# Top-32 attention and a top-1 expert layer: routing the first three batches sooner, ranks beside the one-hot rows, four stacked rows for a slot's choice

## The chip, the cores and the metric

One core of one Trainium2 chip runs the whole program in one launch. The metric is the device time of an execution in microseconds (us), taken as the median of three runs. Engines are named as the profile names them: PE (TensorE, matmuls), DVE (VectorE), ACT (ScalarE), POOL (GpSimd) and SP (SyncE, which here only issues DMAs).

## The reference

```
scores = q @ k^T / sqrt(64)                  # 8 batches, 8 heads, 576 x 576
kth    = 32nd largest score of each row
scores = where(scores >= kth, scores, -1e9)
attn   = softmax(scores)                     # exp(s - max) / (sum + 1e-9)
x      = (attn @ v) as 4608 tokens x 512     # heads side by side

logits = x @ w_gate + modality_bias[modality_id]   # 8 experts
e_idx  = argmax(logits);  gate = softmax(logits)[e_idx]
out    = gate * (relu(x @ w1[e_idx]) @ w2[e_idx])  # w1 512 x 1024, w2 1024 x 512
```

All of it is in float32. A token's expert depends on the attention output of all eight heads, so the tokens of a batch can be routed only when its 36 tiles are done.

## The kernel before

The attention is cut into 32 pairs (a batch and two heads) of 9 query tiles, 288 tiles in all, 36 to a batch. One loop of 310 steps pipelines them: step i multiplies the scores of tile i+2 on PE (`S`, line 383) and transposes the probabilities of tile i-9 (`T`, line 491), while DVE looks for the 32 largest of the tiles in between (lines 395 to 446) and forms the masked probabilities (line 457, or in the first 48 tiles lines 464 and 470 with POOL). PE multiplies by v for three tile roles of a pair (line 519). One 36-step stretch is called a batch period here.

When the attention of a batch is complete, some steps later, small operations of the router are dealt out over the steps, a handful to each step: reciprocals, logits, one-hot rows of the chosen experts (`route`, lines 616 to 622), then in a later step the ranks of the tokens in their experts' lists (`ranks`, lines 599 to 606, PE), the destinations, and the scatter of the x rows to lists in DRAM by five indirect DMAs on POOL (`send`, line 610). `PAUSE` in a list ends the step's share. `done` marks the batch as seen.

The experts work on slots of 256 rows. `sched` chooses the next expert and its rows on DVE (lines 672 to 699, ending in the row `sei`), SP reads `sei` into registers (lines 703 and 706) and issues the DMA of the rows, `xg` (line 707), and of the weights (lines 728 and 732). PE transposes `xg` (line 774 when the list of waiting work is empty, line 786 when the slot before is still running) and does 16 units of x @ w1 (line 796) and 16 of h @ w2 (line 808) in full fp32. These units stand in one list, `moe`; a budget for each step (`STEP`, the costs in `COST`, the cap `CAP`) says how many are taken into PE's instructions behind the attention's. Thirteen slots go into the loop. Slots 0 to 5 are chosen by the long form of `sched` (partly filled lists), 6 to 12 by the short form (`whole`). Where there is no expert work, `keep_warm` (line 960) puts in six bf16 matmuls that nobody reads.

After the loop the tail does six slots one after the other with three fp32r matmuls for each fp32 one (lines 1057 and 1073). Their operands are split into high and low parts on ACT and DVE (lines 1012 and 1013); the choices there are of the long form.

All instructions of an engine run in the order in which they are written, so this planning in Python at build time sets what waits behind what. `arrange` orders the DVE operations within a step by modelled durations; the small operations are one chain there. In steps near the routing of the first seven batches up to `RNQ` of the choice's and `SNQ` of the router's small operations go into one step.

Of the kernel before, what the change touches and what calls it, by code (L numbers as in the profile page):

```python
# [9 lines left out]
FT = mybir.dt.float32  # L10
# [19 lines left out]
NW = 3  # L30
# [14 lines left out]
TL = LR + 2  # L45
# [11 lines left out]
QO = 0  # L57
PJ0 = (1, 2, 3)
FAST = 7
RXQ = (2, 3, 3, 4, 4)  # L60
SNQ, RNQ = 12, 12
RLF = (0, 1)
RXF = (3, 4, 5, 6, 7)
EZP = 1
# [11 lines left out]
def kernel(  # L76
# [132 lines left out]
    base = const.tile([128, E], FT, name="base")  # L209
    er = const.tile([128, 2, E], FT, name="er")  # L210
    G.iota(er[:, 0, :], pattern=[[1, E]], base=0, channel_multiplier=0, allow_small_or_imprecise_dtypes=True)
    roff = er[:, 1, :]
    zc = const.tile([1, 2], FT, name="zc")
    G.memset(zc[:, 0:1], 0.0)
    G.memset(zc[:, 1:2], float(ZROW))
# [371 lines left out]
    def route(lg, bias, oh, x5b, wait=0):  # L587
# [20 lines left out]
        def send(c):  # L608
# [12 lines left out]
            lambda: V.tensor_tensor(oh[:, 0:4, :], key[:, 0:4, :], bc(km)[:, 0:4, :], op=OP.is_equal),  # L621
            lambda: V.tensor_tensor(oh[:64, 4, :], key[:64, 4, :], km[:64, 4:5].to_broadcast([64, E]),
                                    op=OP.is_equal),
            PAUSE,
            *[PAUSE] * wait,
            lambda: A.activation(ez, z, AF.Exp),
            ranks,
            PAUSE,
            lambda: V.tensor_reduce(sm, ez, axis=AX.X, op=OP.add),
            lambda: V.tensor_scalar(sm, sm, EPS, None, op0=OP.add),  # L630
# [25 lines left out]
    def sched(s, whole):  # L656

        o = {"w1": {}}  # L660
        SL[s] = o
        t8 = lambda nm: const.tile([128, E], FT, name=nm)
        av_, key, oh, m8, jk, a8 = t8("s_av"), t8("s_key"), t8("s_oh"), t8("s_m8"), t8("s_jk"), t8("s_a8")
        sc = const.tile([128, 6], FT, name="s_sc")
        at, n_, full, r0, r1 = (sc[:, x:x + 1] for x in range(1, 6))
        i = s % 2
        ei = sei[i]
        mk = smk[i]
        ft = const.tile([128, 2], FT, name="s_ft")
        dot = lambda x, y, w=1.0: V.scalar_tensor_tensor(jk, oh, w, y, op0=OP.mult, op1=OP.mult, accum_out=x)  # L670
        pick = [
            lambda: V.tensor_tensor(av_, base, roff, op=OP.subtract),
            lambda: V.scalar_tensor_tensor(key, av_, float(E), rev, op0=OP.mult, op1=OP.add),
            lambda: V.max(m8, key),
        ]
        if whole:
            both = const.tile([128, 2, E], FT, name="s_er")
            ea = const.tile([128, 2], FT, name="s_ea")
            pick += [lambda: V.tensor_scalar(full, m8[:, 0:1], float(SLOT * E), None, op0=OP.is_gt),
                     lambda: V.tensor_scalar(oh, key, m8[:, 0:1], full, op0=OP.is_equal, op1=OP.mult),  # L680
                     lambda: V.tensor_tensor(both, er, oh[:, None, :].to_broadcast([128, 2, E]), op=OP.mult),
                     lambda: V.tensor_reduce(ea, both, axis=AX.X, op=OP.add),
                     lambda: V.tensor_tensor(ei, ea[0:1, :], zc, op=OP.add)]
        else:
            pick += [lambda: V.tensor_scalar(oh, key, m8[:, 0:1], None, op0=OP.is_equal),
                     lambda: dot(n_, av_),
                     lambda: V.scalar_tensor_tensor(a8, base, -float(SLOT), eoff, op0=OP.add, op1=OP.max),
                     lambda: V.tensor_tensor(a8, a8, roff, op=OP.min),
                     lambda: dot(at, a8),
                     lambda: dot(r0, roff),  # L690
                     lambda: dot(r1, base),
                     lambda: V.tensor_scalar(ft, pos, at, r0, op0=OP.add, op1=OP.is_ge),
                     lambda: V.tensor_scalar(mk, pos, at, r1, op0=OP.add, op1=OP.is_lt),
                     lambda: V.tensor_tensor(mk, mk, ft, op=OP.mult),
                     lambda: dot(sc[:, 0:1], ie),
                     lambda: V.tensor_scalar(ei, sc[0:1, 0:2], float(ZROW), None, op0=OP.add)]
        done = [lambda: V.scalar_tensor_tensor(roff, oh, float(SLOT), roff, op0=OP.mult, op1=OP.add)] if whole else [
            lambda: V.tensor_scalar(n_, n_, float(SLOT), None, op0=OP.min),
            lambda: V.scalar_tensor_tensor(roff, oh, n_, roff, op0=OP.mult, op1=OP.add),
        ]  # L700

        def which():
            o["e"] = SP.value_load(ei[:, 0:1], min_val=0, max_val=E - 1)

        def rows():
            a = SP.value_load(ei[:, 1:2], min_val=0, max_val=ZROW)
            r = SP.dma_start(xg, xs[ds(a, SLOT), :].rearrange("(p t) w -> p t w", t=2)).ins
            o["rows"] = True
# [282 lines left out]
    for x in range(QL):  # L991
# [3 lines left out]
            qk(0, 0, qbd[0])  # L995
            keep_warm(KP)
        sevac(x)
    keep_warm(NW)
    ok = lambda x: 0 <= x < NT
    early = lambda u: u < EARLY and u % 3 != 2  # L1000
    dn_of = lambda u: den[(u // 36) % 2][:, (u // 9) % HP, role(u):role(u) + 1]
# [109 lines left out]
    for i in range(LAST):  # L1111
# [59 lines left out]
        if 0 <= b1 < B:  # L1171
            if r == 0:
                chore.extend(recip(b1, den[b1 % 2]))
# [10 lines left out]
                    xrow(b1, c, xTs(b1), x5)  # L1184
                    cost += COST["xrow"]
            if r == rl[1] + (1 if early_route(b1) else 2):
                steps, store = route(lgb[b1 % 2], bias_all[:, b1], ohb[b1 % 2], x5, int(FAST <= b1 < B - 1))
# [277 lines left out]
```

## Time and profile before

| | us |
|---|---|
| median of 3 runs (lowest, highest) | 1211.64 (1211.17, 1212.91) |
| profiled execution | 1209.28 |
| span in its trace | 1207.6 |
| PE busy | 1157.0 (96%) |
| DVE busy | 1104.1 (91%) |
| ACT busy | 983.4 (81%) |
| POOL busy | 677.7 (56%) |

The span is the stretch between the first and the last instruction in the trace; the rest of the execution's time lies around it. A busy share is a mean over stages, so whichever engine is short has to be read from the windows. In a timeline a row's bracket tells how long the engine sat idle before it and on whom it waited. `SPq` is SP's queue of DMA issues. The granted clock (PEclk) is given as a share of TensorE's full 2.4 GHz; its lower level is 1.2 GHz.

### The profile page before, as it was taken

The page shows a single profiled execution, that of the slowest core. Times are in us where ns is not written, and L with a number is a line of the kernel's source. Part 1 is how long each engine was busy: PE and PEld are TensorE (multiplying, and loading weights), DVE is VectorE, ACT ScalarE, POOL GpSimd, SP SyncE. Part 2 cuts the span into 40 slices and gives each one's busy share as a digit, 9 for nine tenths or more (in the row PEclk, how much of TensorE's full clock was granted, in tenths as well). Part 3 has the DMA queues.
Part 4 walks back from the last instruction along what each step waited for, and adds up shares of the span by engine and source line. Part 5 has one row for each costly group of instructions (what it writes and reads, how often), then busy time and mean ns, then how long its engine had stood idle before and what let it go on. Part 6 is the DMA issues. An engine that isn't in the chain of part 4 may idle for free.

```text
span 1207.6 us, 28111 instructions
## 1 busy us (share of the span) xinstructions
PE 1157.0 (96%) x7920; PEld 906.5 (75%) x7920; DVE 1104.1 (91%) x5562; ACT 983.4 (81%) x2015; POOL 677.7 (56%) x1256
## 2 busy tenths in 40 slices
PE   8889979999999998999999999999999999999998
PEld 6666767778677876878687777868787777589987
DVE  7999999999999999999999999999998999486772
ACT  5999978998888986998899899989998888355652
POOL 6888875564755565565656576556655666121011
PEclk9999999999999998999999999999999999999999
DMA  5653358663586637664675657665675653277750
GB/s 125 174 163 88 88 127 236 191 167 88 153 241 152 164 104 220 175 174 123 174 215 149 168 148 196 168 160 147 183 192 145 177 156 126 83 269 237 261 198 22
DMA packets 204324, 197.10 MB, mean 163 GB/s; under 512 B 104413, under 2 KB 151533, under 8 KB 204160
## 3 DMA queue, kind: packets, MB, share of 16 engines
q1 hardware_dynamic: 196880, 175.92, 54.0%
q0 software_dynamic: 6080, 19.00, 4.3%
q8 instruction: 66, 1.08, 0.4%
q14 instruction: 98, 0.80, 0.2%
q10 hardware_dynamic: 1200, 0.30, 0.1%
HBM read 118.63 MB, written 24.23 MB: 118 GB/s over the span
## 4 chain that ended last, share of the span: by engine, by line
PE 59%; DVE 31%; ACT 5%; issue 2%; DMA 1%; POOL 0%; SPq 0%; POOLq 0%; ACTq 0%; DVEq 0%
PE E L796 11%; PE E L808 11%; PE X L519 8%; DVE cand L395 8%; PE S L383 7%; PE T L491 6%; DVE mg L437 5%; DVE P L457 5%; PE X L1073 5%; PE X L1057 4%; DVE cand L406 2%; DVE cand L407 2%; PE E L1057 1%; DVE mg L408 1%; PE X L317 1%
## 5 line engine op out<-in xcount | busy, mean ns | idle before, releaser
L395 DVE MAX8 cand<-Ssb 128x8 f32<-128x96 f32 x1728 | 388.1, 244 | 1.8 <-ACT Ssb L388 1.8
L433 POOL TENSOR_TENSOR y<-Ssb,K 128x576 f32<-128x576 f32 x288 | 368.7, 1280 | 30.5 <-ACT K L427 30.1
L383 PE MATMUL S<-ks,qs 128*128 128x288 f32 x992 | 221.1, 345 | 18.7 <-ACT Ssb L388 12.9
L427 ACT ACTIVATE K<-Ssb,n 128x576 bf16<-128x576 f32 x288 | 229.9, 798 | 7.3 <-POOL y L433 6.9
L388 ACT ACTIVATE Ssb<-S 128x576 f32<-128x576 f32 x284 | 187.8, 661 | 53.5 <-PE S L383 23.8
L437 DVE MAX8 mg<-y 128x8 f32<-128x576 f32 x288 | 213.3, 741 | 4.2 <-POOL y L433 4.2
L796 PE MATMUL E<-xgT,w1b 128*128 128x256 f32 x832 | 201.1, 384 | 2.6 <-ACT hT L800 1.5
L451 ACT ACTIVATE ex<-Ssb,sm 128x576 f32<-128x576 f32 x256 | 202.3, 790 | 0.0
L383 PEld LDWEIGHTS S<-ks,qs 128*128 128x128 f32 x992 | 152.1, 190 | 66.8 <-issue 26.2
L457 DVE SCALAR_TENSOR_TENSOR P<-Ssb,kth,ex 128x576 f32<-128x576 f32 x230 | 193.7, 842 | 6.8 <-ACT ex L451 5.6
L499 ACT ACTIVATE PT<-T 128x640 f32<-128x640 f32 (+1 forms) x288 | 193.5, 672 | 5.8 <-PE T L491 5.8
L808 PE MATMUL E<-w2b,hT 128*128 128x512 f32 x416 | 194.2, 595 | 0.5 <-ACT hT L800 0.2
L491 PE MATMUL T<-idf,P 128*128 128x128 f32 x1152 | 169.5, 274 | 7.2 <-ACT P L476 6.6
L796 PEld LDWEIGHTS E<-xgT,w1b 128*128 128x128 f32 x832 | 151.0, 190 | 29.5 <-ACT hT L800 7.4
L480 POOL TENSOR_SCALAR spare<-P 1x1 f32<-1x1 f32 x230 | 41.7, 181 | 196.6 <-DVE mg L406 166.7
L519 PE MATMUL X<-PT,vm 128*64 128x256 f32 (+1 forms) x1536 | 147.3, 334 | 1.2 <-DVE x L553 1.2
L491 PEld LDWEIGHTS T<-idf,P 128*128 128x128 f32 x1152 | 137.2, 140 | 13.8 <-ACT P L476 10.7
L519 PEld LDWEIGHTS X<-PT,vm 128*64 128x64 f32 x1536 | 89.1, 138 | 46.4 <-issue 12.5
L420 POOL TENSOR_SCALAR n<-mg 128x1 f32<-128x1 f32 x288 | 71.2, 247 | 92.5 <-DVE mg L408 70.1
L808 PEld LDWEIGHTS E<-w2b,hT 128*128 128x128 f32 x416 | 73.3, 190 | 61.9 <-issue 58.1
L1079 POOL DMA_INDIRECT out_dram<-ot,tk x12 | 12.3, 1022 | 101.9 <-ACT ot L1078 101.9
L427 ACT ACTIVATION_READ_ACCUMULATOR K<-Ssb,n 128x1 f32 x288 | 63.7, 221 | 0.0
(234 smaller groups left out, 2166.1 us busy)
## 6 DMA issues: line engine op xcount, KB each, us to landing
w1b<-in_moe_w_dram SPq DMA_DIRECT2D x76, 512.0 KB, 5.7
w2b<-in_moe_w_dram SPq DMA_DIRECT2D x76, 512.0 KB, 5.1
ks<-st SPq DMA_DIRECT2D x62, 288.0 KB, 4.3
ks<-st SPq DMA_DIRECT2D x62, 256.0 KB, 4.5
qs<-st SPq DMA_DIRECT2D x124, 128.0 KB, 5.3
xg<-xs SPq DMA_DIRECT2D x19, 516.0 KB, 4.1
vm<-in_v_dram SPq DMA_DIRECT2D x32, 256.0 KB, 5.1
km<-in_k_dram SPq DMA_DIRECT2D x63, 128.0 KB, 3.6
```

The costliest lines, as they stand in the source:

```text
L383: PE.matmul(ps[:, hf, :288], l, m, start=(n == 0), stop=(n == len(terms) - 1))
L395: return [lambda s=s: V.max(c[:, s * 8:s * 8 + 8], T[i]["S"][:, bnd[s]:bnd[s + 1]]) for s in range(NSUB)]
L427: A.activation(t["K"], t["S"], AF.Sign, scale=2.0 ** -24 - 1.0, bias=t["n"][:, 1, i % 3:i % 3 + 1], accum_out=t["n"][:, 0, i % 3:i % 3 + 1])
L433: G.tensor_tensor(t["y"], t["S"], t["K"], op=OP.mult)
L437: V.max(t["mg"][:, i % 3, 24:32], t["y"])
L451: A.activation(t["ex"], t["S"], AF.Exp, bias=t["s"][:, i % 3:i % 3 + 1])
L457: V.scalar_tensor_tensor(t["P"], t["S"], kth[:, i:i + 1], t["ex"], op0=OP.is_ge, op1=OP.mult, accum_out=dn)
L491: PE.transpose(T[i]["pt"][:, x, :], (Pm if c == 4 else Pb[c % 2])[:, h * 512 + x * 128:h * 512 + x * 128 + 128], idf)
L499: A.activation(o, T[i]["pt"][:, :n], AF.Copy)
L519: PE.matmul(o.rearrange("p (a b) -> p a b", a=2) if j < 8 else o, l, r, start=(c == 0), stop=(c == 4))
L796: PE.matmul(ps[:, f % 2], w1b[:, c, f * 128:(f + 1) * 128], xgT[:, c, :], start=(c == 0), stop=(c == KC - 1))
L808: PE.matmul(o["py"], hT[:, f, t * 128:(t + 1) * 128], w2b[:, f, :], start=(f == 0), stop=(f == FC - 1))
```

## The change

For the first three batches (`SOON`) the router's schedule counts from one step earlier, the v product of a batch's last role-7 tile is executed at once and not queued, the preparation of k in the second pair of batches 1 to 3 moves from the second step of the pair to the third, the ranks follow the one-hot rows without a pause and stand ahead of the softmax of the gate, and the scatters are handed out by the third x row's step. `RNQ` is 18 where it was 12. In the long form of `sched`, four rows (expert number, list start, list end, last start) are stacked in `er`, so that one product with the one-hot row and one reduction give what five dot products gave. The six warm-up matmuls before the loop are gone.

```
-SNQ, RNQ = 12, 12
+SOON = 3
+SNQ, RNQ = 12, 18
...
+    er = const.tile([128, 4, E], FT, name="er")
+    roff, base, last = (er[:, x, :] for x in range(1, 4))
...
             lambda: V.tensor_tensor(oh[:64, 4, :], key[:64, 4, :], km[:64, 4:5].to_broadcast([64, E]),
                                     op=OP.is_equal),
-            PAUSE,
-            *[PAUSE] * wait,
-            lambda: A.activation(ez, z, AF.Exp),
-            ranks,
+            *[PAUSE] * (wait + 1 - soon),
+            *[lambda: A.activation(ez, z, AF.Exp), ranks][::-1 if soon else 1],
             PAUSE,
...
+        sums = [lambda: V.tensor_tensor(both, er[:, :w], oh[:, None, :].to_broadcast([128, w, E]), op=OP.mult),
+                lambda: V.tensor_reduce(ea, both, axis=AX.X, op=OP.add),
+                lambda: V.tensor_tensor(ei, ea[0:1, 0:w:w - 1], zc, op=OP.add)]
...
-            pick += [lambda: V.tensor_scalar(oh, key, m8[:, 0:1], None, op0=OP.is_equal),
-                     lambda: dot(n_, av_),
-                     lambda: V.scalar_tensor_tensor(a8, base, -float(SLOT), eoff, op0=OP.add, op1=OP.max),
-                     lambda: V.tensor_tensor(a8, a8, roff, op=OP.min),
-                     lambda: dot(at, a8),
-                     lambda: dot(r0, roff),
-                     lambda: dot(r1, base),
-                     lambda: V.tensor_scalar(ft, pos, at, r0, op0=OP.add, op1=OP.is_ge),
-                     lambda: V.tensor_scalar(mk, pos, at, r1, op0=OP.add, op1=OP.is_lt),
-                     lambda: V.tensor_tensor(mk, mk, ft, op=OP.mult),
-                     lambda: dot(sc[:, 0:1], ie),
-                     lambda: V.tensor_scalar(ei, sc[0:1, 0:2], float(ZROW), None, op0=OP.add)]
+            pick += [lambda: V.scalar_tensor_tensor(last, base, -float(SLOT), eoff, op0=OP.add, op1=OP.max),
+                     lambda: V.tensor_scalar(oh, key, m8[:, 0:1], None, op0=OP.is_equal),
+                     lambda: V.tensor_tensor(last, last, roff, op=OP.min)] + sums
...
-            lambda: V.tensor_scalar(n_, n_, float(SLOT), None, op0=OP.min),
+            lambda: V.tensor_scalar(n_, r1, r0, float(SLOT), op0=OP.subtract, op1=OP.min),
+            lambda: V.tensor_scalar(ft, pos, at, r0, op0=OP.add, op1=OP.is_ge),
             lambda: V.scalar_tensor_tensor(roff, oh, n_, roff, op0=OP.mult, op1=OP.add),
+            lambda: V.tensor_scalar(mk, pos, at, r1, op0=OP.add, op1=OP.is_lt),
+            lambda: V.tensor_tensor(mk, mk, ft, op=OP.mult),
...
-    keep_warm(NW)
     ok = lambda x: 0 <= x < NT
...
         part = (PREP if p else PREP0).get(j)
+        if 1 <= p // HP <= SOON and p % HP == 1 and j in (1, 2):
+            part = PREP.get(1) if j == 2 else None
...
-        b1, r = divmod(i - (TL + 2), 36)
+        b1, r = divmod(i - (TL + 1), 36)
+        if b1 > SOON:
+            b1, r = divmod(i - (TL + 2), 36)
         b1 -= 1
+        soon = b1 < SOON
...
-            if r == max(rl[1], rx[4]) + (1 if early_route(b1) else 2):
+            if r == (rx[2] + 1 if soon else max(rl[1], rx[4]) + (1 if early_route(b1) else 2)):
...
-            if role(u) == 7:
+            if role(u) == 7 and not (u % 36 == 35 and u // 36 < SOON):
                 avs.extend(f)
```

What this does to the plan, read from the two builds: for batch 0 the choice of slot 0 stands in step 50 (52 and 53 before), the scatters in steps 50 to 52, the rows' DMA in step 52 (54) and PE's first use of them in step 53 (55), and POOL's product of line 470 no longer stands between the fourth scatter and the fifth. For batch 1 the choice and the rows of slot 2 stand in step 90 (92 and 93), for batch 2 those of slot 4 in step 126 (128 and 129). From there on the list of expert work runs ahead of the kernel before by 4 to 13 elements (a unit is an element).

The first place is SP's queue at the choice of slot 4. In the kernel before, the copies of the next pair's keys (`ks`) stand ahead of the loads of `sei`:

```order
290 L333 DMA ks<-st 64x2x576 x2
291 L333 DMA ks<-st 64x2x512
292 L333 DMA ks<-st 64x2x64
293 L333 DMA ks<-st 64x2x512
294 L333 DMA ks<-st 64x2x64
295 L703 TENSOR_LOAD sei_132
296 L703 ISA x2
297 L706 TENSOR_LOAD sei_132
298 L706 ISA x2
299 L707 ISA
300 L707 DMA xg<-xs 128x1032
```

Now:

```order
292 L699 TENSOR_LOAD sei_132
293 L699 ISA x2
294 L700 ISA
295 L700 DMA xg<-xs 128x1032
296 L721 ISA
297 L721 DMA w1b<-in_moe_w_dram 128x4x256
298 L721 ISA
299 L721 DMA w1b<-in_moe_w_dram 128x4x256
300 L721 ISA
301 L721 DMA w1b<-in_moe_w_dram 128x4x256
302 L333 DMA ks<-st 64x2x576 x2
303 L333 DMA ks<-st 64x2x512
```

The six `ks` issues have moved behind the rows' DMA and three loads of w1.

The second place is PE in step 165, just after slot 6 has been chosen in step 164 (both kernels choose it there). Before, the step's rows are S, T, the transposes of q (line 317) and three units of line 808:

```order
1554 L383 MATMUL S<-ks,qs 128x288 x4
1555 L491 MATMUL T<-idf,P_120 128x128 x4
1556 L317 MATMUL X<-idf,qm 128x128 x4
1557 L808 MATMUL E<-w2b,hT 128x512 x3
1558 L383 MATMUL S<-ks,qs 128x288 x4
1559 L491 MATMUL T<-idf,P_120 128x128 x5
1560 L296 MATMUL X<-st,nid 128x512
1561 L808 MATMUL E<-w2b,hT 128x512 x3
1562 L383 MATMUL S<-ks,qs 128x288 x4
1563 L491 MATMUL T<-idf,P_119 128x128 x4
```

Now (line 801 was 808, line 779 was 786):

```order
1512 L383 MATMUL S<-ks,qs 128x288 x4
1513 L491 MATMUL T<-idf,P_120 128x128 x4
1514 L317 MATMUL X<-idf,qm 128x128 x4
1515 L801 MATMUL E<-w2b,hT 128x512 x2
1516 L779 MATMUL X<-idf,xg 128x128 x4
1517 L801 MATMUL E<-w2b,hT 128x512
1518 L383 MATMUL S<-ks,qs 128x288 x4
```

The first transposes of `xg` for slot 6 stand in step 165 behind two units; before, they stand in step 170.

The third place is PE from the last x rows of batch 7 (line 552) into the tail. Before:

```order
2203 L552 MATMUL X<-idf,xT 128x128 x4
2204 L808 MATMUL E<-w2b,hT 128x512
2205 L552 MATMUL X<-idf,xT 64x128 x4
2206 L786 MATMUL X<-idf,xg 128x128 x4
2207 L808 MATMUL E<-w2b,hT 128x512 x7
2208 L1028 MATMUL X<-idf,xg 128x128 x8
2209 L808 MATMUL E<-w2b,hT 128x512
2210 L1057 MATMUL X<-xgh,w1h 128x256
```

Now (lines 1020 and 1049 were 1028 and 1057):

```order
2160 L552 MATMUL X<-idf,xT 128x128 x4
2161 L801 MATMUL E<-w2b,hT 128x512
2162 L552 MATMUL X<-idf,xT 64x128 x4
2163 L801 MATMUL E<-w2b,hT 128x512 x5
2164 L1020 MATMUL X<-idf,xg 128x128 x8
2165 L1049 MATMUL X<-xgh,w1h 128x256
```

Three units and one set of transposes fewer stand there, and one unit more is gone from the steps ahead of it. On ACT the split of `xg` now stands behind the copy of the last result `ot` and a third split of w1; before it stood ahead of that copy, behind three splits of w1.

## Rows read from the trace of the kernel before

**Rows 1.** The page, parts 1 and 4: busy time; shares of the last chain.

```profile
PE 1157.0 (96%) x7920; PEld 906.5 (75%) x7920; DVE 1104.1 (91%) x5562; ACT 983.4 (81%) x2015; POOL 677.7 (56%) x1256
...
PE 59%; DVE 31%; ACT 5%; issue 2%; DMA 1%; POOL 0%; SPq 0%; POOLq 0%; ACTq 0%; DVEq 0%
```

**Rows 2.** Windows, three batch periods: busy us by engine, granted clock (PEclk), DMA share, GB/s.

```profile
273.06:402.12 129.06, 125.89 (x847) 95.60 (x845) 126.46 (x692) 113.17 (x236) 76.24 (x148) 1.00 0.63 164
402.12:535.92 133.80, 128.25 (x847) 98.36 (x846) 129.66 (x691) 112.66 (x235) 76.44 (x146) 0.97 0.60 164
535.92:664.38 128.46, 126.24 (x854) 97.59 (x853) 125.03 (x659) 113.82 (x236) 78.38 (x152) 1.00 0.60 166
```

**Rows 3.** Timeline of POOL, first scatter: start, us, operation, [idle before, releaser].

```profile
173.44 1.27 POOL L470 TENSOR_TENSOR ex<-Ssb,hT 128x576 f32<-128x576 f32 x1 [0.93 <-DVE hT L464]
...
178.84 1.27 POOL L470 TENSOR_TENSOR ex<-Ssb,hT 128x576 f32<-128x576 f32 x1
180.27 1.28 POOL L610 DMA_INDIRECT xs<-x,dest  x1 [0.15 <-issue]
```

**Rows 4.** Chain of waits, first slot: start, us, what.

```profile
180.27 4.88 DMA xs<-x,dest
...
185.16 3.38 DMA xg<-xs
```

**Rows 5.** Timeline of PE, first use of gathered rows.

```profile
188.69 0.63 PE L774 MATMUL E<-idf,xg 128*128 128x128 f32 x4 [0.81 <-DMA xg<-xs]
```

**Rows 6.** Windows around the first slot and around step 130.

```profile
169.92:188.69 18.77, 11.12 (x78) 8.00 (x75) 16.13 (x100) 11.09 (x26) 14.79 (x25) 0.82 0.50 163
180.85:188.69 7.84, 6.48 (x54) 4.62 (x54) 5.27 (x32) 6.04 (x15) 5.64 (x11) 0.78 0.73 254
455.00:460.00 5.00, 3.62 (x16) 3.04 (x18) 4.97 (x31) 2.46 (x5) 3.33 (x5) 0.55 0.99 279
460.00:465.00 5.00, 5.00 (x24) 2.48 (x21) 4.42 (x23) 1.75 (x4) 2.82 (x7) 0.77 1.14 287
```

**Rows 7.** Timeline of all engines, the choice for slot 4.

```profile
445.53 5.47 SPq L333 DMA_DIRECT2D ks<-st  x6
...
449.86 0.14 DVE L696 TENSOR_SCALAR sei<-s_sc 1x2 int32<-1x2 f32 x1
...
452.94 0.37 SPq L707 DMA_DIRECT2D xg<-xs  x1
...
456.38 1.11 PE L786 MATMUL X<-idf,xg 128*128 128x128 f32 x4 [4.91 <-DMA xg<-xs]
```

**Rows 8.** Timeline of all engines, the choice for slot 6.

```profile
581.69 2.84 PE L808 MATMUL E<-w2b,hT 128*128 128x512 f32 x6
581.82 0.15 DVE L683 TENSOR_TENSOR sei<-s_ea,zc 1x2 int32<-1x2 f32 x1
...
583.37 0.35 SPq L707 DMA_DIRECT2D xg<-xs  x1
```

**Rows 9.** Lines of DVE, choice in the first tail slot: busy us, mean ns.

```profile
L670 DVE SCALAR_TENSOR_TENSOR s_jk<-s_oh,base 128x8 f32<-128x8 f32 x1 | 0.2, 169 | 0.0
...
L670 DVE DVE_READ_ACCUMULATOR s_jk<-s_oh,base 128x1 f32 x1 | 0.1, 84 | 0.0
```

**Rows 10.** Lines of DVE, the choice for slot 6, same columns.

```profile
L681 DVE TENSOR_TENSOR s_er<-er,s_oh 128x16 f32<-128x16 f32 x1 | 0.2, 174 | 0.0
```

**Rows 11.** Timeline of PE, start of the tail.

```profile
1054.06 6.28 PE L808 MATMUL E<-w2b,hT 128*128 128x512 f32 x14
...
1061.51 0.68 PE L1057 MATMUL X<-xgh,w1h 128*128 128x256 f32 x1
```

**Rows 12.** Timeline of ACT, start of the tail.

```profile
1054.69 2.94 ACT L1012 ACTIVATE w1h<-w1b 128x1024 fp32r<-128x1024 f32 x3
1060.81 1.08 ACT L1012 ACTIVATE xgh<-X 128x512 fp32r<-128x512 f32 x2 [3.18 <-PE X L1028]
1062.11 0.69 ACT L818 ACTIVATE ot<-E,sgt 128x512 f32<-128x512 f32 x1 [0.21 <-PE E L808]
```

More of the change, by code (lines that the diff above doesn't have):

```diff
@@ L208 @@
     hT = const.tile([128, FC, SLOT], FT, name="hT")
-    base = const.tile([128, E], FT, name="base")
-    er = const.tile([128, 2, E], FT, name="er")
+    er = const.tile([128, 4, E], FT, name="er")
     G.iota(er[:, 0, :], pattern=[[1, E]], base=0, channel_multiplier=0, allow_small_or_imprecise_dtypes=True)
-    roff = er[:, 1, :]
+    roff, base, last = (er[:, x, :] for x in range(1, 4))
     zc = const.tile([1, 2], FT, name="zc")
@@ L585, in logit_rows, with route @@
                 lg[:r, c0:c0 + n, :], lt[:r].rearrange("p c e a h -> p c e (a h)"), axis=AX.X, op=OP.add))
-    def route(lg, bias, oh, x5b, wait=0):
+    def route(lg, bias, oh, x5b, wait=0, soon=False):
         t5 = lambda nm: const.tile([128, 5], FT, name=nm)
@@ L662, in sched @@
         t8 = lambda nm: const.tile([128, E], FT, name=nm)
-        av_, key, oh, m8, jk, a8 = t8("s_av"), t8("s_key"), t8("s_oh"), t8("s_m8"), t8("s_jk"), t8("s_a8")
-        sc = const.tile([128, 6], FT, name="s_sc")
-        at, n_, full, r0, r1 = (sc[:, x:x + 1] for x in range(1, 6))
+        av_, key, oh, m8 = t8("s_av"), t8("s_key"), t8("s_oh"), t8("s_m8")
+        sc = const.tile([128, 2], FT, name="s_sc")
+        n_, full = (sc[:, x:x + 1] for x in range(2))
         i = s % 2
@@ L669, in sched @@
         ft = const.tile([128, 2], FT, name="s_ft")
-        dot = lambda x, y, w=1.0: V.scalar_tensor_tensor(jk, oh, w, y, op0=OP.mult, op1=OP.mult, accum_out=x)
+        w = 2 if whole else 4
+        both = const.tile([128, w, E], FT, name=f"s_er{w}")
+        ea = const.tile([128, w], FT, name=f"s_ea{w}")
+        r0, r1, at = (ea[:, x:x + 1] for x in range(1, 4)) if w == 4 else (None,) * 3
+        sums = [lambda: V.tensor_tensor(both, er[:, :w], oh[:, None, :].to_broadcast([128, w, E]), op=OP.mult),
+                lambda: V.tensor_reduce(ea, both, axis=AX.X, op=OP.add),
+                lambda: V.tensor_tensor(ei, ea[0:1, 0:w:w - 1], zc, op=OP.add)]
         pick = [
@@ L676, in sched @@
         if whole:
-            both = const.tile([128, 2, E], FT, name="s_er")
-            ea = const.tile([128, 2], FT, name="s_ea")
             pick += [lambda: V.tensor_scalar(full, m8[:, 0:1], float(SLOT * E), None, op0=OP.is_gt),
[L680 to L683, printed above, removed]
-        else:
-            pick += [lambda: V.tensor_scalar(oh, key, m8[:, 0:1], None, op0=OP.is_equal),
-                     lambda: dot(n_, av_),
-                     lambda: V.scalar_tensor_tensor(a8, base, -float(SLOT), eoff, op0=OP.add, op1=OP.max),
-                     lambda: V.tensor_tensor(a8, a8, roff, op=OP.min),
-                     lambda: dot(at, a8),
-                     lambda: dot(r0, roff),
-                     lambda: dot(r1, base),
-                     lambda: V.tensor_scalar(ft, pos, at, r0, op0=OP.add, op1=OP.is_ge),
-                     lambda: V.tensor_scalar(mk, pos, at, r1, op0=OP.add, op1=OP.is_lt),
-                     lambda: V.tensor_tensor(mk, mk, ft, op=OP.mult),
-                     lambda: dot(sc[:, 0:1], ie),
-                     lambda: V.tensor_scalar(ei, sc[0:1, 0:2], float(ZROW), None, op0=OP.add)]
@@ L697, in sched @@
+                     lambda: V.tensor_scalar(oh, key, m8[:, 0:1], full, op0=OP.is_equal, op1=OP.mult)] + sums
+        else:
+            pick += [lambda: V.scalar_tensor_tensor(last, base, -float(SLOT), eoff, op0=OP.add, op1=OP.max),
+                     lambda: V.tensor_scalar(oh, key, m8[:, 0:1], None, op0=OP.is_equal),
+                     lambda: V.tensor_tensor(last, last, roff, op=OP.min)] + sums
         done = [lambda: V.scalar_tensor_tensor(roff, oh, float(SLOT), roff, op0=OP.mult, op1=OP.add)] if whole else [
-            lambda: V.tensor_scalar(n_, n_, float(SLOT), None, op0=OP.min),
+            lambda: V.tensor_scalar(n_, r1, r0, float(SLOT), op0=OP.subtract, op1=OP.min),
+            lambda: V.tensor_scalar(ft, pos, at, r0, op0=OP.add, op1=OP.is_ge),
@@ L1186 @@
             if r == rl[1] + (1 if early_route(b1) else 2):
-                steps, store = route(lgb[b1 % 2], bias_all[:, b1], ohb[b1 % 2], x5, int(FAST <= b1 < B - 1))
+                steps, store = route(lgb[b1 % 2], bias_all[:, b1], ohb[b1 % 2], x5, int(FAST <= b1 < B - 1), soon)
                 side.extend(steps)
```

## The prediction

> **What bounds the kernel now.** I read the page first. PE is busy 96% of the span and DVE 91%, and the chain that ended last runs 59% over PE and 31% over DVE [rows 1]. Neither engine is alone, so what an edit is worth depends on the place. The next view is therefore the windows, cut at batch periods of 36 steps. In an undisturbed period, 535.92 to 664.38, PE works 126.24 of 128.46 us and DVE 125.03: PE sets the pace with DVE 1.2 us behind it [rows 2]. So only what takes idle time or half-speed time from PE shortens such a period; expert work that is done earlier does not, it only moves. Period 402.12 to 535.92 is the odd one: 133.80 us [rows 2]. The timeline inside it shows why: PE waits 4.91 us for the rows of slot 4 [rows 7]. The other bad place is the first slot, where PE is busy 11.12 of 18.77 us [rows 6], and the chain of waits there runs from POOL's last scatter over the rows' DMA to PE [rows 4, 5]. Last comes the tail's start, read from PE's and ACT's timelines [rows 11, 12].
>
> **The first slot.** The rows land at 185.16 + 3.38 = 188.54 [rows 4], and PE begins at 188.69 [rows 5]. The plan puts all of that two steps sooner. A plain step is 128.46 / 36 = 3.57 us [rows 2]; a routing step here, from one product of line 470 to the next, took 178.84 - 173.44 = 5.40 [rows 3]. Two steps are thus 7.1 to 10.8 us. The fifth scatter no longer stands behind a product of 1.27 us on POOL [rows 3], but the steps that are left take over the small operations of the two that go. I take the low end, with these two about even, less half a microsecond: the rows land 6.6 to 7.7 us sooner, at about 181. That is not the gain. What PE did between 180.85 and 188.69, 6.48 us busy [rows 6], is the attention of steps 54 and 55. It now stands behind the wait, not in front of it: 181 + 6.5 against 188.5, a gain of about 1. Against it stands the clock. From 169.92 to 188.69 PE was granted 0.82 [rows 6], so (1 - 0.82) x 18.77 = 3.4 us were lost already; a longer single wait can lose as much again. I take 0, between -1.6 (attention at full speed) and +3.4.
>
> A rule speaks against the change at this point, and it is no part of the sum. After the 4.91 us wait for slot 4 [rows 7] the granted clock was 0.55 and then 0.77 [rows 6]. The Trainium skill, "TensorE: Matmul & The Clock Gate", section "HAM oscillation — how this bites in real kernels", says that a matmul group which waits for a DMA before each slice restarts at half rate each time. The trace agrees in this place. By that rule each DMA wait that the change adds costs more than its idle time, and the first slot would be at its upper end.
>
> **The wait for slot 4 goes.** It came about so: `sei` was ready at 449.86, but SP was issuing six `ks` copies from 445.53 for 5.47 us, so the rows' DMA left at 452.94 and PE, which was there at 456.38 - 4.91 = 451.47, waited [rows 7]. In the change the choice stands three steps sooner, ahead of the `ks` issues, and PE reads the rows two steps after their DMA. The price of the old wait: 4.91 idle, and of the clock (1 - 0.55) x 5 + (1 - 0.77) x 5 = 3.4, of which 0.6 falls on idle time (456.38 - 455.00, at 0.55), so 7.7 at most. Part is taken up by DVE being the later engine just before; the periods tell how much: 133.80 - 128.46 = 5.3 [rows 2]. I take -5.3, bounds -7.7 and -4.9.
>
> **A wait for slot 6 comes.** Both kernels choose slot 6 in step 164. Before, its rows were read five steps later. In the change the list runs ahead, and the first transposes stand in step 165 behind two units. In the trace of before the units of that step begin at 581.69 and three take 2.84 [rows 8], so PE would be there at 581.69 + 1.9 = 583.6. `sei` comes at 581.82, the rows' DMA leaves at 583.37 [rows 8] and takes 3.4 as in the first slot [rows 4]: 586.8. That is a wait of 3.2. Valued like the old one (5.3 paid for 4.91 idle), it costs 3.5. Bounds: 0, if PE is over 3 us later against DVE than it was, and 5.
>
> **Idle time filled.** Slot 2 begins in step 91 and not 95. The period of that slot had 129.06 - 125.89 = 3.2 us of idle PE against 2.2 in the undisturbed one [rows 2], and six keep-warm matmuls that are not in the change. I take -1.5, bounds 0 and -3.2. The warm-up matmuls before the loop I cost at nothing: nobody reads them, and there PE has time to spare before DVE; an estimate of both bounds is 1 us, half of it their own length and half a slower clock behind them.
>
> **The shorter choice.** A dot product is 0.169 + 0.084 = 0.25 us of DVE [rows 9]; five go, 1.27, and two conversions with them. In come a product over 128x32 and a reduction, nearest row 0.174 for 128x16 [rows 10], and a subtraction: net about -0.75 a choice. A fixed price dominates in these rows; were it all per element, the two would be 0.35 each and the net -0.4. Six choices in the loop are 4.5 us of DVE. DVE is the path for 31% [rows 1]: -1.4, bounds 0 and -4.5. In the tail one choice stands ahead of splits that PE waits for: -0.6; the other four are covered by PE's fp32r matmuls.
>
> **The tail.** Four units that the tail's start did are now in the loop. There they cost 6.28 / 7 = 0.90 each [rows 11], 3.6 in all. Do they come back? From the first unit at 1054.06 to the first fp32r matmul at 1061.51 PE needed 7.45 us [rows 11], and with the four transposes ahead of that unit (0.63 as in [rows 5], 0.5 without the overlap) 7.95. In the change it does five units (4.5), then ACT copies the result (0.69), splits w1 (2.94 / 3 = 0.98) and only then `xgh`, whose start lies 1061.51 - 1060.81 = 0.70 ahead of the matmul [rows 12]; with 0.2 of latency 7.1. That is 0.9, and 0.2 for the unit ahead of the x rows. So 1.1 of 3.6 comes back, if the third split is really late: +2.5 against the loop's gain, bounds 0 and +3.6.
>
> **Sum.** 0 - 5.3 + 3.5 - 1.5 - 1.4 - 0.6 + 2.5 = -2.8. On the profiled execution's 1209.28 (span 1207.6 plus 1.7 around it) this gives 1206.5; that execution lies 2.4 under the median of 1211.64, so the median should be 1208.8.
>
> **Rivals.** *Faster: the wait for slot 6 does not come.* PE runs later against DVE once the list never runs dry, and then meets the rows when they are there; the splits in the tail also find ACT free. Without the 3.5 and with half of the tail's 2.5 the sum is -7.6, so 1204. For it: in period 402.12 to 535.92 DVE's 129.66 [rows 2] gives PE room to fall back. Against it: step 164 is one of long DVE work, where PE runs ahead.
>
> *Slower: the first slot pays.* Place: step 53, with everything of steps 54 and 55 behind the wait. Should the rows land only 3 us sooner, since step 50 now carries 18 small operations and the step lasts longer for it, the 6.48 us of attention [rows 6] end 3.5 later than before, and a second half-speed stretch adds up to 3.4. The sum is -2.8 + 6.4 = +3.6, so 1215. It decides from a landing after 188.5 - 6.5 = 182.0. For it: the 5.40 step [rows 3]. Against it: DVE's small operations are the same ones and have only moved.
>
> *No change: it does not do what it says.* The two steps that go are eaten by the two that remain, the lead is small, slot 4 still waits for SP and slot 6 does not. What remains is the shorter choice and a little idle time: -0.5 to -1.5, so 1210.5.
>
> **How the numbers follow.** Forecast 0.43, faster rival 0.24, slower rival 0.17, no change 0.16. Differences of over 0.2% (2.4 us) can be told from none here. The forecast's own range is 1206 to 1211.5, of which 0.26 lies below 1209.2: faster 0.26 + 0.24 = 0.50. Within 0.2% are the rest of the forecast, 0.17, the no-change case at 0.13: 0.30. Slower: 0.17 and 0.03 of a no-change case that also loses the idle stretches: 0.20. The range reaches to the faster rival and halfway through the slower: 1203 to 1214.5.
>
> **What would show it.** In the profile after: rows of slot 0 landing near 181 and PE's S rows behind them at a granted clock under 1; no wait of PE on `xg` near step 128, and period 402 to 536 shortened by about 5; a new wait on `xg` of some 3 us in step 165, with half speed after it; choices of about 0.75 us less on DVE; the first fp32r matmul some 7 us after the last x row. Wrong would be: a wait on `xg` in step 128 as before, a landing of slot 0 after 182, or a loop that is shorter by as much as the units it gained, which would mean that DVE and not PE paid for them.

## The result and the profile after

The changed kernel takes 1222.01 us (median of 7, 1215.86 to 1226.00) where the kernel before took 1211.17 (7 runs, 1209.57 to 1213.59): 1.0075 times as long in the comparison of the runs, 95% interval [1.0056, 1.0093] (the two medians alone give 1.0090). Forecast was 1208.8, with 1203 to 1214.5 as the range: it is slower, and outside. Its runs also lie further apart, 10 us against 4 (7 in the two larger sessions further down, with 19 and 23 runs of the kernel before). The profiled execution took 1222.68 with a span of 1221.0, 13.4 us more than the span of before.

The page after, parts 1 and 4, answers to [rows 1]:

```profile
PE 1160.2 (95%) x7896; PEld 909.8 (75%) x7896; DVE 1101.5 (90%) x5474; ACT 982.6 (80%) x2015; POOL 677.5 (55%) x1256
...
PE 52%; DVE 30%; ACT 7%; DMA 7%; issue 3%; SPq 1%; POOL 1%; POOLq 0%; ACTq 0%; DVEq 0%
```

DVE lost 2.6 us of work. That is the sign that the shorter choice should bring, but not the size: eleven long choices at the forecast 0.75 make 8, and e3 below, with that edit alone, has 1097.1 us, 7.0 less than before. PE has as much to do as before. New is the 7% of DMA in the chain, where it was 1%. The waits of PE name it (us in all, times, longest; line 767 was 774 before, 789 was 796, 1005 was 1013):

```profile
PE S L383 <- DMA qs<-st: 11.4, 5, 3.3
PE E L767 <- DMA xg<-xs: 8.6, 2, 7.8
```

`qs<-st` are the copies of a pair's queries, which SP issues. In the kernel before:

```profile
PE S L383 <- DMA qs<-st: 4.7, 3, 2.3
```

Now the windows cut at DVE's ends of the same steps as in [rows 2], from step 45 on (columns as there):

```profile
144.52:279.30 134.78, 120.90 (x848) 97.71 (x845) 127.91 (x669) 112.05 (x240) 82.13 (x145) 0.95 0.59 162
279.30:406.41 127.11, 125.12 (x846) 95.18 (x846) 124.83 (x675) 113.18 (x236) 74.40 (x148) 1.00 0.62 175
406.41:535.51 129.10, 127.74 (x853) 97.39 (x852) 125.82 (x675) 113.67 (x237) 76.19 (x148) 1.00 0.66 172
535.51:664.72 129.21, 125.37 (x844) 95.57 (x843) 125.02 (x659) 112.34 (x234) 78.05 (x152) 1.00 0.61 168
664.72:795.86 131.14, 128.04 (x852) 98.54 (x852) 126.88 (x660) 113.07 (x236) 77.91 (x151) 0.99 0.60 165
```

A table over all stretches, from the one profiled execution of each kernel (us, between DVE's ends of these steps; the last column runs to the span's end), says where the time went and serves the experiments too. The profiled executions of e1 and e9 are the fastest of their kernels' runs, 4.4 and 6.8 us under the medians, and those of the kernel before, of e5 and of e7 lie 1 to 2 us under theirs; so a difference of two rows is that of two executions, and what an edit is worth is read from the ratios.

| | 45-81 | 81-117 | 117-153 | 153-189 | 189-225 | 225-261 | 261-285 | 285-end |
|---|---|---|---|---|---|---|---|---|
| before | 128.8 | 129.1 | 133.8 | 128.5 | 127.3 | 127.2 | 88.5 | 200.2 |
| after | 134.8 | 127.1 | 129.1 | 129.2 | 131.1 | 129.6 | 91.4 | 204.2 |
| difference | +6.0 | -2.0 | -4.7 | +0.7 | +3.8 | +2.4 | +2.9 | +4.0 |
| e1 | 134.6 | 127.2 | 128.7 | 129.0 | 127.1 | 127.6 | 88.6 | 202.9 |
| e3 | 127.5 | 129.6 | 127.9 | 127.9 | 127.3 | 128.1 | 88.4 | 199.9 |
| e5 | 125.5 | 128.1 | 127.2 | 130.7 | 127.8 | 127.9 | 87.9 | 198.3 |
| e7 | 127.5 | 129.9 | 134.2 | 128.4 | 127.3 | 127.5 | 88.4 | 200.0 |
| e9 | 134.2 | 127.1 | 128.1 | 128.4 | 127.9 | 130.7 | 88.7 | 198.8 |

The losses lie in three places (the first slot, steps 189 to 285, the tail), and the two gains were forecast. PE's timeline after has the rows that make the losses (start, us, operation, idle before and releaser):

```profile
180.17 1.09 PE L767 MATMUL E<-idf,xg 128*128 128x128 f32 x4 [7.83 <-DMA xg<-xs]
...
214.36 0.78 PE L383 MATMUL S<-ks,qs 128*128 128x288 f32 x4 [2.22 <-DMA kqt<-in_k_dram]
...
584.86 0.66 PE L779 MATMUL X<-idf,xg 128*128 128x128 f32 x4 [1.42 <-DMA xg<-xs]
...
730.65 1.30 PE L383 MATMUL S<-ks,qs 128*128 128x288 f32 x4 [2.87 <-DMA qs<-st]
...
861.38 0.77 PE L383 MATMUL S<-ks,qs 128*128 128x288 f32 x4 [2.48 <-DMA qs<-st]
...
992.79 0.77 PE L383 MATMUL S<-ks,qs 128*128 128x288 f32 x4 [3.35 <-DMA qs<-st]
...
1073.34 0.35 PE L1049 MATMUL X<-xgh,w1h 128*128 128x256 f32 x1 [1.38 <-POOL spare L536]
1074.74 0.39 PE L1049 MATMUL X<-xgl,w1h 128*128 128x256 f32 x1 [1.05 <-DVE xgl L1005]
```

The first answers to [rows 5]: the rows of slot 0 land at 180.0 and not 188.5, and PE waits 7.83 us in one piece. Three waits for query copies stand 131 us apart, at the same step of batches 4, 5 and 6, where nothing of `SOON` acts. The row at 214.36 names a load of k; such a wait is put down to what came last by the profile, and in e6 the wait at this place is 4.6 us and names the query copies. The S there reads query copies that SP issued late, as its queue shows (start, us, operation):

```profile
200.94 0.45 SPq L725 DMA_DIRECT2D w2b<-in_moe_w_dram  x1
201.88 0.38 SPq L721 DMA_DIRECT2D w1b<-in_moe_w_dram  x1
203.12 0.35 SPq L700 DMA_DIRECT2D xg<-xs  x1
204.03 0.37 SPq L725 DMA_DIRECT2D w2b<-in_moe_w_dram  x1
205.10 2.42 SPq L335 DMA_DIRECT2D qs<-st  x4
```

In the kernel before, these four copies left 4.9 us sooner, and ahead of slot 1's rows:

```profile
200.23 2.45 SPq L335 DMA_DIRECT2D qs<-st  x4
...
210.97 0.35 SPq L707 DMA_DIRECT2D xg<-xs  x1
```

In windows behind several of these waits the granted clock is down (columns as in [rows 2]):

```profile
180.00:185.00 5.00, 4.83 (x22) 4.74 (x23) 4.91 (x31) 3.22 (x6) 2.48 (x6) 0.55 0.79 261
...
730.00:735.00 5.00, 4.35 (x18) 3.46 (x19) 4.86 (x29) 2.60 (x5) 2.04 (x5) 0.66 0.69 198
...
1073.00:1080.00 7.00, 5.61 (x32) 5.45 (x33) 6.79 (x21) 3.38 (x6) 3.18 (x8) 0.76 0.65 249
```

SP's queue at the choice of slot 8, after and then before, is the comparison to read for batches 4 to 6:

```profile
711.32 0.35 SPq L700 DMA_DIRECT2D xg<-xs  x1
711.88 0.37 SPq L721 DMA_DIRECT2D w1b<-in_moe_w_dram  x1
712.35 5.84 SPq L333 DMA_DIRECT2D ks<-st  x6
718.40 2.88 SPq L721 DMA_DIRECT2D w1b<-in_moe_w_dram  x3
722.03 2.85 SPq L335 DMA_DIRECT2D qs<-st  x4
```

```profile
711.44 0.35 SPq L707 DMA_DIRECT2D xg<-xs  x1
711.89 5.53 SPq L333 DMA_DIRECT2D ks<-st  x6
717.66 1.87 SPq L728 DMA_DIRECT2D w1b<-in_moe_w_dram  x3
719.63 2.62 SPq L335 DMA_DIRECT2D qs<-st  x4
```

The rows' DMA leaves at the same time. In the change a w1 load stands ahead of the key copies, four loads and not three ahead of the query copies, and these leave 2.4 us later. In the chain of waits that end in the S at 730.65, the key copies take 9.31 us and the query copies 7.42; the page's medians from issue to landing are 5.0 and 4.9.

### The profile page after: what moved, and what is told of

Read it like the earlier page. It is cut to its first block, busy times and chain, and to the rows that moved or that the text cites. A ratio compares the mean times of both kernels' runs of the same rounds, so it can differ in the third digit from the quotient of the medians.

```text
span 1221.0 us, 27981 instructions
## 1 busy us (share of the span) xinstructions
PE 1160.2 (95%) x7896; PEld 909.8 (75%) x7896; DVE 1101.5 (90%) x5474; ACT 982.6 (80%) x2015; POOL 677.5 (55%) x1256
## 4 chain that ended last, share of the span: by engine, by line
PE 52%; DVE 30%; ACT 7%; DMA 7%; issue 3%; SPq 1%; POOL 1%; POOLq 0%; ACTq 0%; DVEq 0%
PE E L801 9%; PE X L519 8%; PE E L789 8%; DVE cand L395 8%; PE S L383 6%; PE T L491 5%; DVE P L457 5%; DVE mg L437 5%; PE X L1065 4%; PE X L1049 4%; DMA qs<-st 3%; ACT Ssb L388 2%; DMA ks<-st 2%; DVE cand L406 2%; PE E L1049 1%
## 5 line engine op out<-in xcount | busy, mean ns | idle before, releaser
L457 DVE SCALAR_TENSOR_TENSOR P<-Ssb,kth,ex 128x576 f32<-128x576 f32 x230 | 190.6, 829 | 18.8 <-ACT ex L451 16.2
L801 PE MATMUL E<-w2b,hT 128*128 128x512 f32 x416 | 196.8, 601 | 0.3
L420 POOL TENSOR_SCALAR n<-mg 128x1 f32<-128x1 f32 x288 | 74.7, 259 | 87.1 <-DVE mg L408 64.1
```

Of the source, the lines that this page charges most:

```text
L457: V.scalar_tensor_tensor(t["P"], t["S"], kth[:, i:i + 1], t["ex"], op0=OP.is_ge, op1=OP.mult, accum_out=dn)
L801: PE.matmul(o["py"], hT[:, f, t * 128:(t + 1) * 128], w2b[:, f, :], start=(f == 0), stop=(f == FC - 1))
```

## The experiments

Each kernel ran in five rounds beside the kernel before, whose median in the three sessions was 1211.7 to 1212.7. Between sessions the ratios are to be compared.

**e1: RNQ back to 12 from batch 3 on.**

```
-        for x in range((RNQ if quick else RN) if rush else 0):
+        for x in range(((RNQ if b1 < SOON else 12) if quick else RN) if rush else 0):
```

> The changed kernel with RNQ 18 only for the first three batches and 12 again from batch 3 on; everything else as changed. Theory A (SP's queue by RNQ): with 18 the first w1 load of slots 6, 8, 10, 12 joins the step of the rows' DMA and stands ahead of the key copies, so the query copies land late and PE waits 2.9 + 2.5 + 3.3 us in batches 4 to 6. With 12 those three waits go and the time falls by about 9 to 11 us, to some 1211 to 1213. Theory B (the lead of the expert list is to blame: PE comes sooner and weight buffers come free sooner, so loads fall between the copies whatever RNQ is): the waits stay, within 1 us each, and the time stays at 1219 to 1222.

Measured 1215.73, ratio 1.0030 [1.0017, 1.0044] against 1.0075 for the change: some 5 us less, of 9 to 11 expected. PE's waits from 660 to 1040 say that theory A has the mechanism. For the changed kernel and then for e1:

```profile
PE S L383 <- DMA qs<-st: 8.7, 3, 3.3
```

```profile
PE S L383 <- DMA qs<-st: 0.5, 1, 0.5
```

In the profiled executions the three stretches from step 189 to 285 go from 352.1 to 343.3, to the 343.0 of before, in which PE has no such wait from 660 to 1040. The ratios give less than these 8.8 us. Some of that is chance, since e1's profiled execution is the fastest of its eight. And the waits are not as long in every execution: e9 has the change's order on PE and on SP, instruction by instruction, and in its execution PE waits 5.4 us for query copies there and the three stretches take 347.3.

**e2: RNQ 18 in the kernel before.**

```
-SNQ, RNQ = 12, 12
+SNQ, RNQ = 12, 18
```

> The kernel before with RNQ 18 in place of 12 and nothing else. Theory A: PE gets waits on the query copies in batches 4 to 6 of 2 to 3 us each, and the time rises by 6 to 10 us to 1217 to 1221. Theory B: no such waits, 1210 to 1212, or 1 to 2 us less since slots are loaded a step sooner.

1215.70, ratio 1.0026 [1.0010, 1.0043]: slower by itself, by 3 us and not 6 to 10. From 660 to 1040 PE waits 3.8 us for query copies, longest 2.7, where the kernel before has none. The sign is theory A's, the size half of it.

**e3: the four stacked rows alone.** `sched` and `er` as in the change (their lines of its diff), all else as before.

```
+    er = const.tile([128, 4, E], FT, name="er")
...
+                     lambda: V.tensor_tensor(last, last, roff, op=OP.min)] + sums
```

> The kernel before with the choice by four stacked rows and nothing else (SP's order of loads is as before). My sum gave this part -2 us (1.4 in the loop, 0.6 in the tail), so 1209; both theories expect it to be harmless, between 1207 and 1212. Were it the cause of the loss by itself, it would be over 1215.

1203.11, ratio 0.9926 [0.9913, 0.9940]: 9.5 us faster than before, the surprise of the study, and out of the expected interval on the good side. The two profiled executions differ by 6.7, and in the table 5.9 of it is in 117-153, where slot 4's wait was. In e3's timeline of that place (all engines) PE finds the rows there:

```profile
445.46 0.15 DVE L675 TENSOR_TENSOR sei<-s_ea,zc 1x2 int32<-1x2 f32 x1
...
447.01 0.37 SPq L701 DMA_DIRECT2D xg<-xs  x1
447.48 6.03 SPq L332 DMA_DIRECT2D ks<-st  x6
...
451.08 0.66 PE L780 MATMUL X<-idf,xg 128*128 128x128 f32 x4
```

Against [rows 7]: `sei` is 4.4 us sooner, and the rows' DMA stands ahead of the six key copies and not behind them.

**e4: batches 1 and 2 sooner, batch 0 as before, RNQ 18 for these two** (on e1; the other places of `SOON` likewise).

```
-        if b1 > SOON:
+        if not 1 < b1 <= SOON:
...
-        soon = b1 < SOON
+        soon = 0 < b1 < SOON
```

> The changed kernel with the sooner routing for batches 1 and 2 only (batch 0 as in the kernel before) and RNQ 18 for these two alone. The first period, which is 5.9 us longer in the changed kernel (PE waits 7.8 us for the rows of slot 0 in one piece with the attention of two steps behind it, then 2.2 us for query copies), should be as before. Theory A: waits of batches 4 to 6 gone too, slot 4's wait gone: 1204 to 1208. Theory B: the late waits stay, 1212 to 1217.

1204.82, ratio 0.9937 [0.9923, 0.9951], as theory A had it. But e3 alone gives 1203.11: the sooner routing of batches 1 and 2, with the RNQ of 18 that came with it here, adds nothing to the stacked rows. What either of these two does by itself was not separated.

**e5: slot 0's first use two steps after its rows' DMA** (on e1).

```
-  rush.extend(pick + [begin] + l1[:2] + done + [PAUSE, sent] + rows + go + ...
+  rush.extend(pick + [begin] + l1[:2] + done + [PAUSE, sent] + rows + [PAUSE, PAUSE] + go + ...
```

> The kernel of e1 (changed, RNQ 12 from batch 3 on), with PE's first use of slot 0's rows two steps later (step 55, as in the kernel before), while routing, scatter and the rows' DMA stay two steps sooner. Theory A (order behind the wait: with the use in step 53 PE sits 8 us in front of the attention of steps 54 and 55): PE does that attention while the rows are under way, the wait of 8.3 us falls below 1, the period from step 45 to 81 shrinks from 134.2 to 126 to 128, and since the lead of the list is gone, the wait at the tail's first fp32r matmul (1.4 + 1.0 us and half speed after it) goes too: 1202 to 1206. Theory B (the loss comes from the crowded routing steps 48 to 50): the period stays at 132 to 135 and the time at 1212 to 1216.

1200.89, ratio 0.9909 [0.9888, 0.9931], under the 1202 to 1206 of theory A and 1.2% under e1 with nothing but two pauses between them. PE's first use, in its timeline:

```profile
185.29 0.29 PE L519 MATMUL X<-PT,vt 128*64 128x64 f32 x4
185.51 0.65 PE L767 MATMUL E<-idf,xg 128*128 128x128 f32 x4
```

No wait: the attention of steps 54 and 55 lies where the wait was. The stretch 45-81 is 125.5 against e1's 134.6, the tail 198.3 against 202.9, and e1's 2.1 us wait for copies at the place of 214.36 is gone as well. Theory B falls. A price appears in step 165, where PE waits 3.8 us for slot 6 and the changed kernel has 1.42:

```profile
571.60 0.36 SPq L700 DMA_DIRECT2D xg<-xs  x1
...
578.40 0.66 PE L779 MATMUL X<-idf,xg 128*128 128x128 f32 x4 [3.82 <-DMA xg<-xs]
```

It has the size that the prediction worked out (3.2) but not its cause. PE is no sooner here than in the change, 4.5 us behind `sei` against 3.8; the rows take 6.8 us from the start of their issue to their use, where the change needs 3.4 (581.42 to 584.86). Why they took twice as long was not followed.

**e6: the first w1 load behind the key copies, RNQ 18.**

```
-  rows + rest + l1[:1] + done + [PAUSE, l1[1], l1[2], PAUSE, l1[3]]
+  rows + rest + done + [PAUSE] + l1[:1] + [l1[1], l1[2], PAUSE, l1[3]]     # from batch 3 on
```

> The changed kernel with RNQ 18 throughout; from batch 3 on the first w1 load of a chosen slot stands one step later, behind the key copies, so that four loads stand between the key and the query copies (one ahead of the keys and three between before this edit, three between in e1). If what hurts is a load ahead of the key copies, the three waits of batches 4 to 6 (8.7 us) go: 1213 to 1216, as e1. If it is the number of 512 KB loads ahead of the query copies, four are as many as in the changed kernel: the waits stay at 2 to 3 us each and the time at 1219 to 1223.

1218.29 (1211.83 to 1224.17), ratio 1.0048 [1.0029, 1.0067], between the two expectations. From 660 to 1040 PE waits for copies and loads twice:

```profile
PE S L383 <- DMA w1b<-in_moe_w_dram: 2.3, 1, 2.3
...
PE S L383 <- DMA qs<-st: 0.3, 1, 0.3
```

2.6 us, of 8.7 in the change and 0.5 in e1. That points to the load ahead of the keys for most of it, with the fourth load ahead of the queries for the rest, but it is not shown: the ratio's interval overlaps both the change's and e1's, and e9, with the change's own order, waits 5.4 us. In this execution 45-81 took 140.2 with a 4.6 us wait for query copies, so its time also shows how much that stretch varies.

**e7: e3 with the rows' DMA one step later** (slots 1 and up).

```
-  rush.extend(pick + [begin] + rows + rest + ...
+  rush.extend(pick + [begin] + [PAUSE] + rows + rest + ...
```

> The kernel of e3 (before, with the choice by four rows), with the rows' DMA of slots 1 and up put one step after the choice, behind the key copies. The edit of e3 gave -9.5 us against -2 forecast, and its trace has no wait for the rows of slot 4. Theory C (most of it is that wait: nine operations and the DMA fit into one step of 12, so the rows leave a step sooner and ahead of the keys): the wait of 4 to 5 us comes back and the time rises to 1208 to 1211. Theory D (it is DVE's time in the choices): 1203 to 1205.

1210.43, ratio 0.9987 [0.9974, 1.0000]: theory C. The rows' DMA is back behind the key copies and PE's wait is back, in its timeline:

```profile
456.74 1.11 PE L780 MATMUL X<-idf,xg 128*128 128x128 f32 x4 [5.54 <-DMA xg<-xs]
```

117-153 is 134.2 again, and no other stretch differs from e3's by over 0.6 us. So of the 9.5 us of the stacked rows some 7 are the place of the rows' DMA in SP's queue, nearly all of it slot 4's. The 1 to 2 that are left are in keeping with what the prediction gave to DVE (2.0), though the interval reaches to no gain at all.

**e8: e3 with one w1 load ahead of the query copies and three behind** (while a slot is running).

```
-  l1[:1] + done + [PAUSE, l1[1], l1[2], PAUSE, l1[3]]
+  done + [PAUSE] + l1[:1] + [PAUSE, PAUSE] + l1[1:]
```

> The kernel of e3 with only one w1 load of a chosen slot ahead of the query copies, the other three behind them (three ahead in e3). By the theory that the number of loads ahead of the query copies sets PE's waits on them, these fall from 5.9 us to 2 to 4 us and the time by 1 to 4 us, to 1199 to 1202. If the loads then come late for the slot's first units, PE waits on w1 instead and the time is 1203 or more.

1201.66, ratio 0.9902 [0.9882, 0.9922]. The waits fell from 5.9 to 2.4 us as expected; against e3's 0.9926 the intervals overlap, so a gain of 1.5 to 3 us is likely and not shown.

**e9: the tail's splits in the old order on ACT** (on the changed kernel).

```
-        if i >= CLOSE:
+        for _ in range((i >= CLOSE) * 2):
             in_advance()
```

> The changed kernel, in which two (not one) of the tail's early splits may be placed per step at the end of the loop. The only effect on ACT is that the third split of w1 and both splits of xg stand ahead of the last result's copy, as in the kernel before; PE's order is the same. Theory (the lead makes the loop end with that copy ahead of the splits, and the tail pays for it): the waits of the first fp32r matmuls (1.4 and 1.05 us) shrink below 0.8 together, the half-speed stretch behind them goes, and the stretch from 1060 to the end is 2 to 4 us shorter: 1217.5 to 1220. If the tail's loss has another cause, the time stays at 1221 to 1223.

1215.95, ratio 1.0035 [1.0021, 1.0049], under the 1217.5 to 1220 expected. The last stretch went from 204.2 to 198.8, more than the 2 to 4 expected. ACT after the change and then in e9:

```profile
1071.12 0.69 ACT L811 ACTIVATE ot<-E,sgt 128x512 f32<-128x512 f32 x1 [7.81 <-PE E L801]
1071.71 1.05 ACT L1004 ACTIVATE w1h<-w1b 128x1024 fp32r<-128x1024 f32 x1
1072.65 1.07 ACT L1004 ACTIVATE xgh<-X 128x512 fp32r<-128x512 f32 x2
```

```profile
1052.71 2.95 ACT L1004 ACTIVATE w1h<-w1b 128x1024 fp32r<-128x1024 f32 x3
1061.26 1.09 ACT L1004 ACTIVATE xgh<-X 128x512 fp32r<-128x512 f32 x2 [5.60 <-PE E L801]
1062.23 0.69 ACT L811 ACTIVATE ot<-E,sgt 128x512 f32<-128x512 f32 x1
```

In the change ACT sat idle for 7.81 us and then had the copy and a split ahead of `xgh`. In e9 PE's waits there are 0.30 and 0.32 and the clock stays at 1.00. From the first unit behind the x rows (1066.63, in e9 1056.33) to the end of the span it is 154.4 us in the change and 151.1 in e9, so 3.3 of the 5.4 us are the order on ACT. The other 2.1 lie ahead of that place. PE's timeline there, after the change and then in e9, both behind the same wait of 1.37 us for DVE:

```profile
1061.48 3.38 PE L801 MATMUL E<-w2b,hT 128*128 128x512 f32 x4
```

```profile
1052.88 1.88 PE L801 MATMUL E<-w2b,hT 128*128 128x512 f32 x4
```

The granted clock is 0.71 in the change (1060.30 to 1066.20) and 1.00 in e9 (1051.70 to 1056.30). e6, which has the change's order on ACT and the same 1.37 us wait, is at 1.00 there too, and its last stretch takes 200.8. So this piece does not come in every execution.

**e10: e5 with e8's loads from batch 3 on.** Both edits as above.

> e5 with e8's edit from batch 3 on: one w1 load of a chosen slot ahead of the query copies, three behind. e5 has 1.2 us of waits on query copies in batches 4 to 6; with these gone it should come to 1199 to 1201. If the two edits don't add up, it stays at 1201 or more.

1203.18, ratio 0.9930 [0.9915, 0.9945]: no gain on e5, the edits don't add up, and why was not followed further.

**e11: e8 with batch 0 alone sooner and e5's two pauses** (the other places of `SOON` likewise).

```
-        soon = b1 < SOON
+        soon = b1 == 0
```

> e8's loads with the sooner routing for batch 0 alone, slot 0's first use two steps after its rows' DMA, RNQ 18 in batch 0 and 12 elsewhere; batches 1 and 2 as in the kernel before. e4 against e3 says that the sooner routing of batches 1 and 2 brings nothing (1204.8 against 1203.1), e5 against e4 that the sooner batch 0 with the later use brings 3.9. So 1201.7 - 3.9 = 1197.8, range 1196 to 1200. If the gain of e5 hung on batches 1 and 2 as well, 1200 to 1202.

1199.13, ratio 0.9897 [0.9881, 0.9913]: faster than both kernels of the study, 1% under the one before. Against e8 (0.9902) the sooner batch 0 is not told apart from nothing by the medians; its stretch 45-81 is 125.5 where e8 has 127.5.

## Why the prediction was wrong, point by point

*Two steps were wrong in what they left out.* Nearly every sign that the prediction named came true (the landing, slot 4, the tail's 7 us), and the time was wrong all the same: 13.4 us more in the profiled executions against the forecast -2.8. Two places make 15.1 of these 16.2 us, +6.0 in the first slot and +9.1 by `RNQ`.

"The first slot" counted the wait and the clock, and put 0, between -1.6 and +3.4. The landing was right (180.0 for "about 181"), the clock fell as named (0.55), and PE's S of steps 57 to 61 stands 1.5 to 2.6 us later than before, inside the bounds though not at 0. Part of that is a misread row: the 6.48 us from 180.85 on are step 55 alone, since PE's S of step 54 ran at 175.45, and in the change step 54's rows (3.0 us before, at the low clock) stand behind the wait as well. The larger part is that the step ended there. With the expert list ahead, slot 1's rows and weight loads came ahead of a pair's query copies in SP's queue (205.10, before at 200.23), PE waited 2.2 more, and with a granted clock of 0.66 behind it (214 to 219) the stretch came to +6.0. e5 shows the cause: two pauses that put the attention of two steps under the wait take back 9.1 us of e1's stretch.

The other omission is the larger: `RNQ` was priced nowhere outside the first three batches, though it acts up to batch 6. With 12, the choice, the rows' DMA and the start flag fill a step exactly, and the first w1 load falls into the next step, behind the key copies. With 18 it goes ahead of them. Cost in the profiled execution 3.8 + 2.4 + 2.9 = 9.1, of which e1's execution takes back 8.8; by the ratios e1 takes back some 5 us, and e2 shows `RNQ` alone to cost 3 in the kernel before. Which of the moved loads does it stays open (e6). The rows of SP's queue at slot 4 that stand with the change show such a regrouping; the prediction used them for the rows' DMA alone and did not ask what else had moved in that queue.

*The sum's other terms.* Slot 4's wait: forecast -5.3, measured -4.7 in its stretch, and the wait is gone. Right for this kernel, but in part by luck: e3 and e7 show that the shorter choice does it alone, by bringing the rows' DMA into the same step; the sooner routing, to which the prediction gave it, was not needed. Slot 6's wait: forecast 3.2 us and +3.5, measured 1.42 and +0.7; right in place and sign, the size off because PE arrived 3.8 us behind `sei` (forecast 1.8), and the half speed that was to follow did not come. Idle time of slot 2: forecast -1.5, measured -2.0. The shorter choice: -2.0 as DVE time, with which e7 agrees (1.3 by the medians, 0 to 3 by the interval); its effect on the order, the 7 us between e7 and e3, was missed. The tail: forecast +2.5 against the loop's gain, and the first fp32r matmul comes 6.7 us after the first unit behind the x rows (1073.34 - 1066.63; forecast 7.1). But the second matmul waited too, and a stretch at 0.76 of the clock followed: +4.0 where the tail's two terms gave +1.9. By e9 3.3 us of the change's last stretch are the order on ACT, waits and clock together; another 2.1 are the slow units ahead of it, which e6 and e9 do not have.

*The rivals.* The slower rival had the right place and the wrong condition: the rows landed sooner than its limit of 182.0, and the slot cost time all the same. The rule of the Trainium skill, "TensorE: Matmul & The Clock Gate", section "HAM oscillation — how this bites in real kernels", that a matmul group which waits for a DMA before each slice restarts at half rate each time, was held outside the sum. The trace bears it out behind four new waits (0.55 after 7.83 us, 0.66 after 2.22 and after 2.87, 0.79 after 3.35), though not behind all: after the 1.42 us in step 165 and after the 2.48 us at 861.38 the clock was 1.00.

## What to carry to other kernels

A queue that issues in order is a resource like an engine: before costing an edit that changes how many operations go into a step, list what stands ahead of what in each DMA queue, through the whole run and not only in the stages the edit is meant for. Starting a consumer sooner than its data moves the wait in front of work that used to hide it; bring the data sooner and leave the use where it was (e1 against e5). A shortened chain can be worth more by what it lets into the same step than by its own time, so try the parts of a joint change alone. And one profiled execution is one draw: before two traces are subtracted, see where each lies among its kernel's runs.

## What was not expected of the hardware

After a wait of 2.87 us PE came back at a granted clock of 0.66 (730 to 735), and after one of 2.48 us at 1.00 (861 to 866). The same wait of 1.37 us ahead of the tail was followed by 0.71 in the change and by 1.00 in e6 and e9, so the length of the wait alone does not settle it. The copies of queries, with four 512 KB loads issued among them and the keys, took 7.42 us to land in the chain at 730, where the median of the page is 4.9. And the change and e9, with the same order on PE, SP and POOL, took 872.3 and 865.1 us over steps 45 to 285: a program that is the same up to there differs by 7 us between two executions. The change's runs spread over 10 us and e3's, with shorter waits on copies, over 2; that transfers which land about when they are needed make the time vary would fit this, but it is not shown, and what sets the time from run to run stays open.
